# Own-segment blocks instead of full 128-key tiles in the token stage of a gated-attention backward kernel

## The chip, the cores and the metric

The kernel runs on one core of a Trainium2 chip. The metric is the device time of one execution in microseconds (us). A group of four heads of one 128-token tile, called a group below, is the unit of work in the stage that is changed.

## The reference, cut to what matters

The function returns the output of a gated sum of two attentions and the gradients of its inputs. Branch A is multi-query attention over 2048 tokens. Branch B is the one that the change touches: the 2048 tokens are cut into 64 segments of 32; each segment attends to itself (causally) and to 8 memory rows, and the attention's output at the memory rows becomes the memory of the next segment.

```python
M, seg = (8, 32)
for s in range(n_seg):
    h = jnp.concatenate([mem, xs], axis=1)
    q, k, v = (jnp.einsum('btd,dhe->bhte', h, W) for W in (Wq, Wk, Wv))
    scores = jnp.einsum('bhqe,bhke->bhqk', q, k) * scale
    p = _softmax(jnp.where(mask[None, None], scores, -1e9), axis=-1)
    o = jnp.einsum('bhte,hed->btd', jnp.einsum('bhqk,bhke->bhqe', p, v), Wo)
    mem = o[:, :M, :].copy()
```

There are 32 heads of 128 dimensions. Backward needs, for each head, P (the softmax), dP = dO V^T, dS = P (dP - delta) x scale with delta the row sum of P times dP, and then dQ = dS K, dK = dS^T Q, dV = P^T dO. The row sum of P times dP equals the row sum of dO times o.

## The kernel before, in words

The program goes through stages that follow one another on the core:

- preparation and projections, which write q, k, v and dO of all tokens to DRAM;
- the forward recurrence over 64 segments (memory rows only), woven with branch A's first pass;
- the token stage (`b_bulk`), which does the attention of the 2048 tokens, forward and backward up to dQ, now that all memories are known;
- the backward recurrence over 64 segments (`b_chain_bwd`), woven with branch A's second pass (`a_pass2`). Beside its own work it computes dK and dV of the last 11 token tiles (`kv_load`, `kv_mm`, `kv_out`, 176 products of four heads);
- the post stage (`b_post`): dK and dV of the other token tiles (`st_KV`), transposes (`st_T`) and the product with the transposed weights (`st_H`), 48 groups;
- the weight gradients (`b_dw`) and the rest of branch A.

Helpers record the instructions: `mm` (L82 of the profile) is every matmul and `tr` (L87) every transpose on TensorE, `evac` (L77 on VectorE, L79 on ScalarE) is a copy out of PSUM. `tp` is the position of a tile of the array: with weights of 128 rows by 32 columns, `tp=(0, 32c)` is one of four column tiles.

A 128-token tile holds four segments. In the token stage of before, a head's scores are a full matrix of 128 tokens by 128 keys, of which the four 32x32 blocks on the diagonal count, and beside it 128 tokens by 32 memory columns (four segments of 8), of which each token's own 8 count. After the exponential a mask of bits (`maskX`, 160 columns) sets everything else to zero. So `x_S` and `x_D` are 128x512 for four heads, `x_P` and `x_dS` 128x512, and `x_m`, `x_Pm`, `x_dSm` 128x128.

The stage runs 128 groups (16 tiles by 8) through a software pipeline that is written out by hand: the list `order` holds pairs of a lag and a step, and iteration t does each step for the group t minus its lag, in the list's order. The steps of before:

- `st_QT`, `st_KT`, `st_GT` (dO), `st_VT`: four transposes each on TensorE and one copy;
- `st_S` (L757 on): four matmuls of own keys, four of memory columns, two exponentials (L765, L766); `st_M`: the mask (L771); `st_R`: row sums (L778), reciprocal (L780), and P on GpSimd (L783, two operations);
- `st_T`: P transposed, 128x512 by 32x32 blocks on VectorE (L727) and the memory part by a transpose on TensorE;
- `st_O` with `attend`: the output of four heads: one matmul of 512 columns with a block-diagonal tile of memory rows (`x_vmB`), then four of 128, and a copy (L737);
- `st_OT`: o transposed, and `x_prod`, dO times o, on GpSimd (L806); `st_B`: the output projection, 8 matmuls of 288 columns, summed over a tile;
- `st_D`: dP, with delta subtracted inside PSUM by matmuls of `x_prod` with a tile of -1 (`negones`), then dS on VectorE (L842, two operations);
- `st_DT`, `st_Q`: as `st_T` and `st_O`, with dS and k; `st_K`: memory gradients, 16 matmuls every second group (L870 copies them).

`load` brings chunks of four groups from DRAM, `after` says behind which lag a chunk's next load is issued, `store` and `flush` put stores on SyncE's queue one iteration late. PSUM has eight banks: two buffers `x_tr`, one each of `x_S`, `x_po`, `x_D` and `x_m`, and two banks of `x_b`.

## Time and profile before

| what | value |
|---|---|
| median of three timed runs | 5509.4 us (5500.12 to 5520.96) |
| the profiled execution | 5481.23 us |
| its span, first to last instruction | 5479.5 us |
| mean granted TensorE clock | 0.982 |
| busy: TensorE (PE), VectorE (DVE), ScalarE (ACT), GpSimd (POOL) | 93%, 68%, 64%, 42% of the span |
| token stage, first transpose of q to the last copy of dQ | 2097 to 2778 us |
| the same, steady part, 2300 to 2500 us | 40 groups; PE busy 92%, DVE 83%, ACT 82%, POOL 53%, DMA engines 82% |

Times come from one profiled execution. The windows view gives each engine's busy time in a stretch of the span; the timeline gives starts and lengths of single instructions or runs of equal ones, with the shape of weights (rows times columns) and of the moving operand. A matmul's length is modelled and overlaps that of the next, so the distance between starts says what one costs.

### The profile page before, as it was taken

To read this page: it belongs to the slowest core of one execution; us is meant where nothing else is said; L and a number is where in the kernel's file an instruction comes from. 1 tells how busy PE (TensorE), PEld (TensorE's weight loads), DVE (VectorE), ACT (ScalarE), POOL (GpSimd) and SP (SyncE) were. 2 spreads that over 40 slices of the span, in tenths; PEclk is the share of its full clock that TensorE was granted. 3 is DMA by queue.
4 is the path that set the end of the run, shared out by engine and by line. 5 is a ranking of instruction groups with operands and counts; after the bars stand their busy time and mean duration, and the time that the engine had idled before them with its cause. 6 is when DMAs were issued, how large, how long until landed. Compare 5 with 4: busy or idle time off the path is not lost. (4 is left out here: it accounts for less than half of the span.)

```text
span 5479.5 us, 213173 instructions
## 1 busy us (share of the span) xinstructions
PE 5110.2 (93%) x90992; PEld 3046.4 (56%) x91173; DVE 3708.4 (68%) x6812; ACT 3496.5 (64%) x5264; POOL 2317.8 (42%) x4450
## 2 busy tenths in 40 slices
PE   8999999999999998999979999999998889999998
PEld 6435555555555556777735555555554457764444
DVE  5337888888888887888868888888888851111112
ACT  4327788888888886888857888788787742111001
POOL 4004555555555545555534454445444421122223
PEclk9999999999999998999989999999999999999999
DMA  6647667776675556888876899999986679976653
GB/s 216 230 175 139 139 133 138 144 136 137 140 140 123 119 105 189 258 254 255 250 242 168 202 210 207 204 211 211 204 193 137 147 165 281 265 225 219 199 174 108
DMA packets 1093581, 1013.05 MB, mean 185 GB/s; under 512 B 636979, under 2 KB 905788, under 8 KB 1083027
## 3 DMA queue, kind: packets, MB, share of 16 engines
q1 hardware_dynamic: 989010, 752.12, 57.2%
q0 software_dynamic: 100016, 242.38, 15.4%
q8 instruction: 713, 11.68, 0.9%
q10 hardware_dynamic: 3600, 4.90, 0.3%
q14 instruction: 242, 1.97, 0.1%
HBM read 547.90 MB, written 383.13 MB: 170 GB/s over the span
## 5 line engine op out<-in xcount | busy, mean ns | idle before, releaser
L1743 DVE TENSOR_TENSOR a_W<-a_dP,a_E 128x512 bf16<-128x512 f32 x2048 | 1315.0, 684 | 251.5 <-issue 118.6
L1889 DVE TENSOR_TENSOR b_dS<-b_dP,b_E 128x512 bf16<-128x512 f32 x2048 | 1311.6, 683 | 248.1 <-issue 115.0
L1866 ACT ACTIVATE b_E<-b_S 128x1024 bf16<-128x1024 f32 x1024 | 1049.1, 1024 | 299.8 <-PE b_dP L82 230.4
L1710 ACT ACTIVATE a_E<-a_S 128x1024 bf16<-128x1024 f32 x1024 | 1050.2, 1026 | 252.1 <-PE a_dP L82 166.7
L82 PEld LDWEIGHTS <-b_QS 32*128 32x128 bf16 (+1 forms) x8192 | 257.3, 92 | 553.2 <-issue 479.1
L82 PE MATMUL b_S<-b_KV,b_QS 32*128 32x512 bf16 x2048 | 406.3, 387 | 101.4 <-ACT b_E L1866 66.2
L82 PE MATMUL r_pj<-WT,r_dT 128*32 128x288 bf16 x12288 | 495.2, 288 | 5.1 <-issue 5.1
L82 PE MATMUL w_acc<-w_d,w_h 128*128 128x512 bf16 (+1 forms) x2352 | 471.0, 379 | 2.5
L82 PE MATMUL a_S<-a_QD,l_KV 32*128 32x512 bf16 x2048 | 401.6, 383 | 55.3 <-ACT a_E L1710 37.9
L82 PE MATMUL b_acc<-b_dS,b_QS 128*32 128x512 bf16 x2048 | 428.0, 396 | 0.9 <-issue 0.8
L82 PE MATMUL a_acc<-a_E,l_VK 128*32 128x256 bf16 x8192 | 403.8, 274 | 9.7 <-issue 5.5
L82 PE MATMUL b_acc<-b_E,b_QS 128*32 128x512 bf16 x2048 | 410.3, 396 | 0.1
L82 PE MATMUL b_dP<-b_KV,b_QS 32*128 32x512 bf16 x2048 | 405.2, 391 | 0.2 <-DVE b_dS L1889 0.2
L82 PE MATMUL a_dP<-a_QD,l_KV 32*128 32x512 bf16 x2048 | 400.6, 387 | 0.1
L82 PEld LDWEIGHTS <-r_dT 128*32 128x32 bf16 x12288 | 333.2, 97 | 101.2 <-issue 9.7
L82 PEld LDWEIGHTS <-w_h 128*128 128x128 bf16 (+1 forms) x2688 | 230.0, 100 | 258.2 <-issue 6.6
L82 PE MATMUL a_acc<-a_W,l_WK 128*32 128x256 bf16 x4096 | 305.6, 283 | 3.8 <-DVE a_W L1743 2.1
L82 PEld LDWEIGHTS <-l_KV 32*128 32x128 bf16 x4096 | 153.9, 91 | 261.6 <-issue 215.7
L79 ACT CAST w_o<-w_acc 128x512 bf16<-128x512 f32 x54 | 31.7, 586 | 384.2 <-PE w_acc L82 362.3
L783 POOL TENSOR_TENSOR x_P<-x_E,x_r 128x512 bf16<-128x512 bf16 x128 | 152.6, 1192 | 293.0 <-DVE x_r L780 290.5
L77 DVE CAST w_o<-w_acc 128x512 bf16<-128x512 f32 x54 | 37.3, 691 | 333.4 <-PE w_acc L82 306.8
L82 PEld LDWEIGHTS <-hm 128*32 128x32 bf16 x7680 | 201.7, 97 | 79.5 <-issue 11.7
(465 smaller groups left out, 10993.8 us busy)
## 6 DMA issues: line engine op xcount, KB each, us to landing
b_QS<-qs_dram SPq DMA_DIRECT2D x256, 256.0 KB
dOx_dram<-p_tok SPq DMA_DIRECT2D x16, 1024.0 KB
c_vx<-vx_dram SPq DMA_DIRECT2D x64, 256.0 KB
krow_dram<-c_k POOLq DMA_DIRECT2D x64, 256.0 KB
qrow_dram<-c_q POOLq DMA_DIRECT2D x64, 256.0 KB, 3.3
vrow_dram<-c_v POOLq DMA_DIRECT2D x64, 256.0 KB, 3.9
x_q<-qx_dram SPq DMA_DIRECT2D x32, 512.0 KB
x_k<-kx_dram SPq DMA_DIRECT2D x32, 512.0 KB
```

What stands on the lines that cost most here:

```text
L77: nc.vector.tensor_copy(out, in_)
L79: nc.scalar.copy(out, in_)
L82: return self.nc.tensor.matmul(out, lhsT, rhs, start=start, stop=stop, tile_position=tp, skip_group_check=True)
L783: nc.gpsimd.tensor_tensor(out=o[:, r, :], in0=Et[:, :, lo:lo + n], in1=rl[:].unsqueeze(2).to_broadcast([P, 4, n]), op=ALU.mult)
L1710: nc.scalar.activation(E_[n][:], S.pop(n)[:], ACT.Exp, scale=SCALEA)
L1743: nc.vector.tensor_tensor(out=W_[n][:, i, :], in0=dP[i][:], in1=E_[n][:, i, :], op=ALU.mult)
L1866: nc.scalar.activation(E_[n][:], S.pop(n)[:], ACT.Exp, scale=SCALEA)
L1889: nc.vector.tensor_tensor(out=D_[n][:, i, :], in0=dP[i][:], in1=E_[n][:, i, :], op=ALU.mult)
```

## The change

A head's scores, P and dS become 32 own keys and 32 memory columns, that is 2 x 32 columns a head in tiles `[P, 2, 4, 32]` (part, head, column). The own-key scores are computed as four 32-column tiles a head, each token segment against its own keys only. The mask has 2 x 32 columns. P^T and dS^T come from one transpose by blocks on VectorE, memory part included. The products P x V, dS x K and, in the later stages, dS^T Q and P^T dO are done by a new helper `diag_mm`: four matmuls on 32x32 tiles at the array's diagonal. Memory rows are loaded to partitions 40r to 40r+8 as whole rows. Delta is the row sum of P times dP times scale, taken on VectorE, and subtracted on GpSimd (`st_Y`); `x_prod` and the matmuls with -1 go from this stage. `st_B` is cut in two halves, the lags and the order of the steps are new, `x_po` has two buffers, `x_m` is gone (memory gradients share a bank with dP), and the loop has 7 extra iterations where it had 9. P and dS are kept in DRAM without their zero blocks.

```diff
-        self.px_dram = t("px_dram", [NTT, P, HB, P])
-        self.dsx_dram = t("dsx_dram", [NTT, P, HB, P])
+        self.px_dram = t("px_dram", [NTT, P, HB, SEG])
+        self.dsx_dram = t("dsx_dram", [NTT, P, HB, SEG])
...
+    def diag_mm(self, out, i, lhsT, rhs, start, stop):
+        for r in range(4):
+            b = slice(32 * r, 32 * r + 32)
+            self.mm(out[b, i, :], lhsT=lhsT[b], rhs=rhs[b], start=start, stop=stop, tp=(32 * r, 32 * r))
...
         def attend(o, PT, m, v):
-            po = psum.tile([P, 4, P], F32, name="x_po", bufs=1)
-            self.mm(po[:].rearrange("p i e -> p (i e)"), lhsT=PT[:, 512:640], rhs=m.rearrange("p i e -> p (i e)"),
-                    start=True, stop=False)
+            po = psum.tile([P, 4, P], F32, name="x_po", bufs=2)
             for i in range(4):
-                self.mm(po[:, i, :], lhsT=PT[:, 128 * i:128 * i + 128], rhs=v[:, i, :], start=False, stop=True)
+                self.diag_mm(po, i, PT[:, 0, i, :], v[:, i, :], True, False)
+                self.diag_mm(po, i, PT[:, 1, i, :], m[:, i, :], False, True)
             nc.scalar.copy(o, po[:])
...
+        def score(t, ps, l4, r4, w, part):
+            tt, g, r, d = view(t)
+            for i in range(4):
+                if part:
+                    self.mm(ps[:, 1, i, :], lhsT=l4[:, i, :], rhs=mT[tt][w][:, :, 4 * g + i, :])
+                    continue
+                for c in range(4):
+                    b = slice(32 * c, 32 * c + 32)
+                    self.mm(ps[b, 0, i, :], lhsT=l4[:, i, b], rhs=r4[:, i, b], tp=(0, 32 * c))
...
         def st_D(t):
...
+            ps = sc["D"][:, 0]
+            score(t, ps, sc.pop(("dOT", t)), sc.pop(("vT", t)), "v", 0)
+            X = sc["X", t] = sp.tile([P, 2, 4, 32], F32, name="x_X", bufs=2)
+            nc.vector.scalar_tensor_tensor(out=flat(X[:]), in0=flat(ps), scalar=SCALEB, in1=flat(d["P"][:, t % 4]),
+                                           op0=ALU.mult, op1=ALU.mult)
+            dl = sc["dl", t] = sp.tile([P, 4], F32, name="x_dl", bufs=2)
+            nc.vector.tensor_reduce(out=dl[:], in_=byh(X[:]), axis=AX.XY, op=ALU.add)
+
+        def st_Y(t):
+            tt, g, r, d = view(t)
+            Y = sp.tile([P, 2, 4, 32], F32, name="x_Y", bufs=1)
+            nc.gpsimd.tensor_tensor(out=Y[:], in0=d["P"][:, t % 4], in1=bc(sc.pop(("dl", t))[:]), op=ALU.mult)
+            o = chunk(t, "dS", [P, 4, 2, 4, 32], 3)
+            nc.gpsimd.tensor_tensor(out=o[:, t % 4], in0=sc.pop(("X", t))[:], in1=Y[:], op=ALU.subtract)
+            store(t, self.dsx_dram, o)
...
-        order = [(0, st_QT), (1, st_S), (3, st_T), (4, st_O), (0, st_KT), (2, st_R), (1, st_M), (5, st_OT), (5, st_VT),
-                 (6, st_D), (0, st_GT), (7, st_B), (8, st_DT), (9, st_Q), (7, st_K)]
+        order = [(0, st_QT), (2, st_GT), (3, st_T), (6, st_B0), (0, st_KT), (2, st_VT), (2, st_R), (6, st_B1), (5, st_OT),
+                 (4, st_Y), (5, st_DT), (1, st_Sm), (3, st_Dm), (1, st_S), (3, st_D), (6, st_K), (1, st_M), (4, st_O),
+                 (6, st_Q)]
...
-        for t in range(NG + 9):
+        for t in range(NG + 7):
```

In the backward recurrence `kv_mm`, and likewise `st_KV` in the post stage, does the token part first, by `diag_mm`, and the memory part after it:

```diff
             for i in range(4):
-                self.mm(pk[:, i, :], lhsT=kvS[rg, i, w, :], rhs=kvR[rg, w, i, :], start=True, stop=False, tp=(rg.start, 0))
+                self.diag_mm(pk, i, a[:, i, :], b[:, i, :], i == 0, False)
             for i in range(4):
-                self.mm(pk[:, i, :], lhsT=a[:, i, :], rhs=b[:, i, :], start=False, stop=True)
+                self.mm(pk[:, i, :], lhsT=kvS[rg, i, w, :], rhs=kvR[rg, w, i, :], start=False, stop=True, tp=(rg.start, 0))
```

In the forward recurrence two loops of eight matmuls, `c_v` by `PBm` and `c_vx` by `PBx`, become one loop that does both for each of the eight heads.

## The prediction

> **What bounds the kernel now.** I read the windows view first, to find the stages that the diff touches and what is busiest in each. Then the order of PE's instructions in them, since the change rewrites matmuls. The columns of the windows are: length, then busy time and count on PE, on the weight loader (PEld), DVE, ACT and POOL, then granted clock, DMA share, GB/s.

> ```profile
> 2300.00:2500.00 200.00, 183.90 (x2823) 152.17 (x2849) 166.33 (x362) 164.80 (x380) 105.75 (x120) 1.00 0.82 254
> 3000.00:4460.00 1460.00, 1375.19 (x29229) 739.14 (x29225) 1229.57 (x2136) 1154.85 (x1516) 675.74 (x1240) 0.99 0.87 190
> 4460.00:4690.00 230.00, 222.19 (x2319) 178.45 (x2320) 40.80 (x112) 54.84 (x101) 31.36 (x56) 0.96 0.94 249
> ```

> The first row is the token stage (2097 to 2778 us), the second the backward recurrence, the third the post stage. PE is the busiest engine in all three; DMA is high too. In the token stage the count of groups in the first window (40) gives 5.0 us a group; the first and the last transposes of q, 2097.0 and 2738.1, give 641.1 / 127 = 5.05 over the whole stage.

> The timeline of PE shows starts (first column) and modelled lengths. I go by starts: a length includes about 0.17 us of pipeline that the next matmul overlaps.

> ```profile
> 2500.72 0.38 PE L82 MATMUL x_po<-x_vmB,x_PT 128*128 128x512 bf16 x1
> 2500.94 0.39 PE L82 MATMUL x_po<-x_v,x_PT 128*128 128x128 bf16 x4
> 2501.16 0.39 PE L87 MATMUL x_tr<-identB,x_k 128*128 128x128 bf16 x4
> ...
> 2502.73 0.26 PE L82 MATMUL x_m<-x_vmT,x_dOT 128*128 128x32 bf16 x4
> 2502.83 0.25 PE L82 MATMUL x_m<-negones,x_prod 128*128 128x32 bf16 x4
> ...
> 2503.15 1.14 PE L82 MATMUL x_b<-WoN,x_oT 128*128 128x288 bf16 x8
> 2504.13 0.22 PE L87 MATMUL x_tr<-identB,x_dSm 128*128 128x128 bf16 x1
> 2504.41 0.39 PE L82 MATMUL x_po<-x_k,x_DT 128*128 128x128 bf16 x4
> 2504.72 0.25 PE L82 MATMUL x_m<-x_q,x_dSm 128*32 128x128 bf16 x4
> 2504.79 0.24 PE L82 MATMUL x_m<-x_dO,x_Pm 128*32 128x128 bf16 x4
> 2504.84 0.24 PE L82 MATMUL x_m<-x_q,x_dSm 128*32 128x128 bf16 x4
> 2504.90 0.24 PE L82 MATMUL x_m<-x_dO,x_Pm 128*32 128x128 bf16 x4
> 2505.07 0.40 PE L87 MATMUL x_tr<-identB,x_q 128*128 128x128 bf16 x4
> ```

> Prices from it: a full 128-column matmul 0.055 us (0.22 / 4), 512 columns 0.22, 288 columns 0.122 (0.98 / 8), full weights with 32 columns 0.027, a 128-column matmul on a 32-column tile 0.015 (0.18 for 12). A change of the tile shape costs 0.09 going in (2504.41 + 0.22 to 2504.72) and 0.11 going out.

> By these a group costs PE now: 20 transposes 1.10, S and D with `negones` 12 x 0.055 = 0.66, their memory columns 12 x 0.027 = 0.32, two memory transposes 0.11, P x V and dS x K 2 x (0.22 + 0.22) = 0.88, output projection 0.98, memory gradients and their switches every second group 0.22. Sum 4.27 us; the other 0.73 of the 5.0 is waiting (0.40 of it recorded as idle, PE busy 183.9 of 200; the rest behind modelled ends). So the stage is PE's work plus in-order waits, on evacuations for the most part.

> **The change, part by part, in the token stage** (128 groups).

> *Own-key scores.* S and D become 16 matmuls each, weights 128x32, 32 columns, on four column tiles. The nearest rows are in the backward chain:

> ```profile
> 3021.10 0.36 PE L82 MATMUL r_x<-r_dOT,r_vxT 128*32 128x8 bf16 x32
> 3021.31 0.42 PE L82 MATMUL r_x<-r_dOT,r_vmT 128*8 128x8 bf16 x32
> 3021.57 0.26 PE L82 MATMUL r_x<-r_prod,negones 128*32 128x64 bf16 x8
> ```

> 32 with 8 columns start within 0.21 us (0.007 each); 8 with 64 columns last 0.26, of which about 0.20 is one (0.009 each). With 128 columns it was 0.015. I take 0.009: 32 x 0.009 = 0.29 us, bounds 0.22 and 0.48.

> [...]

> *P x V and dS x K.* Each becomes 32 matmuls of 128 columns on 32x32 tiles at the diagonal (own keys, then memory), 64 a group. No 32x32 tile and no two row tiles writing one PSUM bank are in the trace of before, so this is the open price. Nearest from below: 128 columns on four column tiles, 0.015 (64 x 0.015 = 0.96 us, against 0.88 now). For row tiles side by side the chain has these:

> ```profile
> 3004.51 0.39 PE L82 MATMUL b_S<-b_KV,b_QS 32*128 32x512 bf16 x2
> 3004.52 0.39 PE L82 MATMUL b_dP<-b_KV,b_QS 32*128 32x512 bf16 x2
> 3004.84 0.39 PE L82 MATMUL b_acc<-b_dS,b_QS 128*32 128x512 bf16 x2
> ```

> Four row tiles start within about 0.01 us and the next work comes 0.33 later: they run together, though into different banks. From above: one after another, 0.055 (3.52 us). I take 0.015, since a diagonal tile shares neither rows nor output partitions with its three neighbours, and both kinds of neighbours are shown to overlap; the other end is a rival.

> *The rest on PE.* 20 transposes 1.10, projection 0.98 and memory columns 8 x 0.027 = 0.22 stay; memory gradients 8 x 0.015 = 0.12; `negones`, `prod` and the two memory transposes go. The new order puts all full-array work first, then column tiles, then diagonal tiles: three switches, 0.09 to 0.12 each, 0.32. Sum: 1.10 + 0.98 + 0.22 + 0.29 + 0.12 + 0.96 + 0.32 = **3.99 us** (bounds with the diagonal at 0.015: 3.92 and 4.18).

> *Other engines.* DVE per group now: transposes 0.70 and 0.70, reduction 0.81, mask 0.46, 0.68 + 0.28 for dS, two copies 0.42, reciprocal 0.18: 4.66. Halved lengths, by straight lines through the rows (0.28 at 128 and 0.68 at 512 elements give 0.41 at 256): 2 x 0.43 + 0.42 + 0.26 + 0.41 + 0.42 for the new delta sum + 0.85 + 0.18 = 3.4. ACT: five 512-element copies of 0.59 and two of 256 at about 0.38 = 3.7, from 4.7; the copies' starts can be 0.49 apart, so it holds a group in about 3.1. POOL: three operations at 0.66 (0.395 at 128, 1.196 at 512) = 2.0, from 2.7, of which two now stand between D and the store of dS, but with an iteration to spare. None of them passes PE.

> *DMA.* In the steady window the dynamic queue moved 34,483 packets and 50.36 MB at 81.7%, 76 ns a packet of 1,460 B; in 700 to 900 us it was 34.5 ns at 356 B. A line through both gives 21 ns + 0.037 ns a byte: 174 ns at 4,096 B, 31 ns at 256 B. Per four groups P and dS change 256 packets of 4,096 B for 1,024 of 256 B, and the memory rows 1,024 of 256 B for 64 of 4,096 B: 44.5 - 31.7 + 31.7 - 11.1 = 33 engine-us less, 0.5 us a group on 16 engines. DMA falls from 4.1 to 3.6 us a group: still under PE, but the next limit. SP issues as many transfers as before.

> *Waits.* Walking one iteration of the new order by these prices, the third transpose group has its buffer free (q copied out by 0.92 us, needed at 0.93), the fourth waits about 0.1 for ACT's copy of dO behind the copies of o and dq, the fifth none. The output buffer of the attention is doubled, which removes the wait between dS x K and P x V. I put waits at 0.25 in place of 0.73: **4.25 us a group**, bounds 4.0 and 4.7. Gain: (5.02 - 4.25) x 128 = 99 us, and two iterations fewer in the tail, at some 4 us, 8 us.

> **Other stages.** Post stage (48 groups, 4.48 us from start to start, all PE): 8 full matmuls (0.44) become 32 diagonal ones (0.48) and one more switch (0.1): 0.14 x 48 = +7 us; its smaller loads of p and dS free DMA, which only two short waits ask for. Backward chain: 176 products, 4 full matmuls (0.22) become 16 (0.24), but the products now end in the shape of the next matmul, b_S, so a switch goes: -0.08 x 176 = -14 at most. Its steps come every 1.555 us, set by b_S, the exponential (1.03 us) and b_S's single buffer, so I count 0, bounds -14 and +10. In the forward chain the pairs are only interleaved: eight matmuls of 0.027 now stand behind one POOL result, whose waits now add up to 1.7 us in 64 steps; I count 0, bounds 0 and +12. Masks and constants at the start: three short POOL operations, under 2 us.

> **Sum.** -99 - 8 + 7 = -100 us. The profiled execution took 5481.2 us (span 5479.5), the median of the three timed runs is 5509.4, 28 above; the sum goes to 5381 for a profiled run, and 5409 against the median.

> **Rivals.**
> 1. *Diagonal tiles run one after another.* Then 0.055 for each: token stage 64 x 0.040 = +2.56, so 6.8 us a group, +228 us against now; chain 16 x 0.040 x 176 = +113, since those steps are already full; post stage 32 x 0.040 x 48 + 7 = +68. About 5509 + 228 + 113 + 68 - 8 = 5910. It decides from 0.027 a matmul on (64 x 0.012 = 0.77 eats the gain): at 0.0275, two at a time, the time is about 5509 + 4 + 35 + 26 - 8 = 5566. For: no row shows row tiles in one bank. Against: the overlap rows above. Chance 0.14.
> [...]
> 2. *The waits stay.* PE gets lighter, yet two transpose buffers and ACT's order keep 0.7 us: 4.7 us a group, -41 - 8 + 7 = -42, 5467. For: five evacuations still share two buffers. Against: the walk above. Chance 0.12.
> 3. *DMA takes over.* Stage at 4.9 to 5.0 us a group because small packets cost twice my line: 5490 to 5510. Against: under 0.5 us of 200 went to DMA waits. Chance 0.08.
> Forecast: 0.66.

> Faster by over 0.5% (27 us; about what a measurement can tell): forecast and rival 2, 0.78. Within: rival 3, 0.08. Slower: rival 1, 0.14. The range runs from period 4.0 without loss elsewhere (-130 - 8 - 14 = -152, near 5355) to rival 3 (5500).

> **What would show it.** Steps: 16 diagonal matmuls of one tile within about 0.24 us; S and D starts 0.007 to 0.015 apart; period 4.25; PE idle under 0.3 us a group; DMA share near 0.85. Wrong if the x_po groups last 1.8 us each, or if a group of transposes is regularly preceded by a wait over 0.3 us.

## The result, and the profile after

The changed kernel is slower: 5591.7 us, the median of four timed runs (5581.83 to 5613.6), against 5515.2 for the kernel before timed beside it (5500.12 to 5524.32). The ratio is 1.0147, with a 95% interval of 1.0105 to 1.0189. The forecast was 5409 us.

The windows view of the profiled execution (span 5580.1 us, clock 0.975), in the columns used before. The first window is the same steady part of the token stage; the other two are shifted by 80 and 100 us, since the later stages now begin about 100 us later:

```profile
2300.00:2500.00 200.00, 158.28 (x5033) 131.60 (x5033) 120.15 (x327) 124.97 (x255) 68.95 (x108) 0.95 0.64 191
3080.00:4540.00 1460.00, 1376.51 (x31144) 735.70 (x31132) 1231.55 (x2136) 1156.76 (x1518) 675.72 (x1235) 0.99 0.84 180
4560.00:4790.00 230.00, 226.94 (x3528) 178.42 (x3517) 41.62 (x115) 55.32 (x103) 32.26 (x58) 0.98 0.84 209
```

In the token stage every engine is busy for less of the time than before, and so is DMA. The stage lost its bound and became slower: something waits. The counts of PE and PEld rose from some 2,830 to 5,033 each. From the first transposes of q to the last, the stage takes 711.4 us where it took 641.1: 5.60 us a group instead of 5.05.

The other stages moved little. Between the spans lie 100.6 us, for the most part:

- +70 in the token stage;
- +28 ahead of it, 27 of them in the forward recurrence (1674.5 us against 1647.7);
- +4 in the backward recurrence (1641.2 against 1637.1);
- nothing in the post stage (218.4 against 218.9).

The timeline of PE in the steady part (start, length, operation, shape of weights, shape of the moving operand, count; in brackets the idle time ahead and what ended it):

```profile
2399.89 0.24 PE L82 MATMUL x_S<-x_kT,x_qT 128*32 128x32 bf16 x10
2401.63 0.22 PE L82 MATMUL x_S<-x_kT,x_qT 128*32 128x32 bf16 x6 [1.49 <-issue]
2401.68 0.27 PE L82 MATMUL x_D<-x_vT,x_dOT 128*32 128x32 bf16 x16
2402.53 0.24 PE L82 MATMUL x_D<-x_q,x_dS 128*32 128x128 bf16 x4 [0.58 <-DVE x_X L846]
2402.59 0.24 PE L82 MATMUL x_D<-x_dO,x_P 128*32 128x128 bf16 x4
2402.76 0.23 PE L82 MATMUL x_po<-x_v,x_PT 32*32 32x128 bf16 x4
2402.82 0.23 PE L82 MATMUL x_po<-x_vmB,x_PT 32*32 32x128 bf16 x4
2402.88 0.23 PE L82 MATMUL x_po<-x_v,x_PT 32*32 32x128 bf16 x4
...
2403.61 0.23 PE L82 MATMUL x_po<-x_kmB,x_DT 32*32 32x128 bf16 x4
2403.76 0.40 PE L87 MATMUL x_tr<-identB,x_q 128*128 128x128 bf16 x4
...
2406.33 0.27 PE L82 MATMUL x_S<-x_kT,x_qT 128*32 128x32 bf16 x16
2406.45 0.26 PE L82 MATMUL x_D<-x_vT,x_dOT 128*32 128x32 bf16 x16
2407.32 0.24 PE L82 MATMUL x_D<-x_q,x_dS 128*32 128x128 bf16 x4 [0.62 <-DVE x_X L846]
```

Three things are to be read here. The diagonal tiles are cheap: groups of four start 0.055 us apart, 0.014 a matmul. There is a wait in nearly every iteration (114 times in 2100 to 2800 us): the memory gradients of `st_K` write the tile `x_D` while VectorE (`x_X`, L846) still reads dP in the other half of it. And there is a hole of 1.49 us in the middle of 16 equal matmuls, which waits for nothing that the profile knows. The largest waits of PE, 2300 to 2500 us (total us, times, longest us):

```profile
PE x_D L82 <- DVE x_X L846: 23.2, 36, 1.0
PE x_tr L87 <- issue: 5.1, 2, 3.1
PE x_tr L87 <- DVE x_kT L77: 4.6, 9, 0.5
PE x_po L82 <- issue: 3.8, 4, 1.6
PE x_S L82 <- issue: 2.2, 2, 1.5
```

In the kernel before the token stage has no wait of the "issue" kind on PE. After has 35 of them with 52.9 us in 2100 to 2800 us. (For every kernel below, such holes are counted in this window for the token stage's tiles.)

**Where the holes lie.** They are at one place of the instruction stream, not of the program. Number PE's instructions in the order of the trace (two for each weight load with its matmul, one for each semaphore instruction). All 35 holes of after then stand at an index that leaves 194 on division by 256, and so do all of k_last (64), k_tr (68), split (32), nomem (19) and light (48), the kernels of the next section; in hyb 32 of 36 stand at 194 or 195. So PE stops where one block of 256 instructions ends and the next begins. The DMA queues of before and of after in 2300 to 2500 us (packets, MB, share of the 16 engines):

```profile
q1 hardware_dynamic: 34483, 50.36, 81.7%
q8 instruction: 22, 0.36, 0.7%
```

```profile
q1 hardware_dynamic: 27106, 37.60, 62.8%
q8 instruction: 38, 0.62, 1.3%
```

A packet of the instruction queue is 16.4 KB, which for 256 instructions is 64 bytes each. Over the whole execution after moves 806 such packets; PE's 103,056 matmuls and 103,141 weight loads make 805.5 blocks of 256. Before it was 713 for 711.6. So this queue carries PE's instructions, and the change nearly doubled what it has to bring in the token stage.

The trace also shows when a block comes. There is one packet a block, in order, and it starts about when PE enters the block ahead of it or later. In after (2150 to 2650 us) the start comes 2.0 us behind that entry at the median, and over 3.8 us behind it in one case of ten; the packet then takes 1.0 us, and PE begins no block sooner than 1.2 us after its packet has landed. That makes 4.2 us at the median and 6 in the late cases, where 256 instructions last 4.4 us at the pace of an undisturbed iteration. In before the delays are much the same (1.9 and 4.3 us), but a block lasts 8.9 us, so none is late.

**What a hole leaves behind.** A hole costs more than its own length, because TensorE's granted clock drops behind many of the long ones. Three windows of after, around the longest hole (columns as above; the clock is the third number from the end):

```profile
2293.60:2298.30 4.70, 0.30 (x5) 0.21 (x3) 0.77 (x2) 0.31 (x1) 0.00 (x0) 1.00 0.67 201
2298.30:2301.70 3.40, 2.89 (x19) 2.04 (x17) 1.26 (x4) 1.17 (x2) 0.88 (x2) 0.50 0.50 180
2301.70:2306.00 4.30, 3.65 (x138) 3.10 (x136) 2.10 (x6) 2.81 (x6) 1.04 (x2) 1.00 0.12 32
```

In the second window four projection matmuls take 0.87 us (2298.18 to 2299.05) that take 0.49 elsewhere. Behind its first 45 us, the token stage of after has 15 such drops, 72 us in all at a granted clock of 0.5; each began with PE idle for 1.7 us or more of the 3.4 us ahead. The same part of before has none.

### The profile page after: what moved, and what is told of

Same layout as the page of the kernel before. It is cut to its first block, busy times and chain, and to the rows that moved or that the text cites. A ratio compares the mean times of both kernels' runs of the same rounds, so it can differ in the third digit from the quotient of the medians.

```text
span 5580.1 us, 237075 instructions
## 1 busy us (share of the span) xinstructions
PE 5102.7 (91%) x103056; PEld 3020.0 (54%) x103141; DVE 3599.7 (65%) x6813; ACT 3407.3 (61%) x4944; POOL 2228.4 (40%) x4453
## 5 line engine op out<-in xcount | busy, mean ns | idle before, releaser
L1878 ACT ACTIVATE b_E<-b_S 128x1024 bf16<-128x1024 f32 x1024 | 1048.2, 1024 | 302.2 <-PE b_dP L82 216.9
L82 PEld LDWEIGHTS <-b_QS 32*128 32x128 bf16 (+1 forms) x8192 | 267.4, 92 | 541.9 <-issue 495.1
L82 PE MATMUL r_pj<-WT,r_dT 128*32 128x288 bf16 x12288 | 492.3, 286 | 11.3 <-issue 11.2
L82 PE MATMUL b_S<-b_KV,b_QS 32*128 32x512 bf16 x2048 | 406.1, 385 | 89.1 <-ACT b_E L1878 65.0
L82 PE MATMUL w_acc<-w_d,w_h 128*128 128x512 bf16 (+1 forms) x2352 | 470.9, 379 | 2.5
L82 PE MATMUL a_S<-a_QD,l_KV 32*128 32x512 bf16 x2048 | 404.1, 385 | 49.3 <-ACT a_E L1722 35.5
L82 PE MATMUL b_acc<-b_dS,b_QS 128*32 128x512 bf16 x2048 | 426.5, 395 | 2.9 <-issue 1.5
L82 PE MATMUL a_acc<-a_E,l_VK 128*32 128x256 bf16 x8192 | 407.0, 276 | 9.3 <-issue 5.1
L82 PE MATMUL b_acc<-b_E,b_QS 128*32 128x512 bf16 x2048 | 408.9, 395 | 0.4 <-issue 0.4
L82 PE MATMUL b_dP<-b_KV,b_QS 32*128 32x512 bf16 x2048 | 406.5, 390 | 2.8 <-issue 2.6
L82 PE MATMUL a_dP<-a_QD,l_KV 32*128 32x512 bf16 x2048 | 402.6, 389 | 0.1
L82 PEld LDWEIGHTS <-r_dT 128*32 128x32 bf16 x12288 | 330.5, 97 | 107.7 <-issue 16.1
L82 PEld LDWEIGHTS <-w_h 128*128 128x128 bf16 (+1 forms) x2688 | 229.8, 100 | 258.4 <-issue 6.6
L82 PE MATMUL a_acc<-a_W,l_WK 128*32 128x256 bf16 x4096 | 306.4, 284 | 6.0 <-issue 5.4
L82 PEld LDWEIGHTS <-l_KV 32*128 32x128 bf16 x4096 | 149.8, 91 | 263.5 <-issue 222.3
L794 POOL TENSOR_TENSOR x_P<-x_E,x_r 128x256 bf16<-128x256 bf16 x128 | 78.5, 614 | 442.8 <-ACT x_vT L79 295.2
L82 PEld LDWEIGHTS <-hm 128*32 128x32 bf16 x7680 | 202.7, 97 | 79.6 <-issue 11.2
```

Of the source, the lines that this page charges most:

```text
L82: return self.nc.tensor.matmul(out, lhsT, rhs, start=start, stop=stop, tile_position=tp, skip_group_check=True)
L794: nc.gpsimd.tensor_tensor(out=o[:, t % 4], in0=Et[:], in1=bc(rl[:]), op=ALU.mult)
L1878: nc.scalar.activation(E_[n][:], S.pop(n)[:], ACT.Exp, scale=SCALEA)
```

## The experiments

Two theories are tested, and they need not exclude each other. **Tile**: the wait of `st_K` for VectorE, 0.61 us in every iteration, is the loss. **Supply**: 280 PE instructions a group, where there were 145, are more than is brought in time beside the stage's transfers; the time at half clock is counted to it where it follows a hole. A third, **forward recurrence**: the interleaved loop costs the 28 us ahead of the stage.

The table gathers the runs. "Instructions" are PE's in a group, as built. "Undisturbed" is the lower quartile of the distance between iterations. "Wanted" is instructions by that distance, the rate that the iteration asks for while nothing is late. "Half clock" is the time at a granted clock of 0.5 in the stage behind its first 45 us.

| kernel | ratio to before | token stage, us | instructions | undisturbed, us | wanted, per us | DMA share | holes, us (count) | half clock, us |
|---|---|---|---|---|---|---|---|---|
| before | 1 | 641 | 145 | 4.94 | 29 | 0.82 | 0 | 0 |
| hyb3 | 0.9983 [0.9967, 1.0000] | 636 | 200 | 4.79 | 42 | 0.72 | 4 (9) | 7 |
| nomem | 0.9978 [0.9962, 0.9993] | 615 | 216 | 4.50 | 48 | 0.76 | 16 (19) | 20 |
| hyb | 0.9917 [0.9888, 0.9946] | 627 | 224 | 4.46 | 50 | 0.75 | 34 (36) | 20 |
| split | 1.0149 [1.0121, 1.0177] | 701 | 260 | 5.02 | 52 | 0.76 | 31 (32) | 14 |
| after | 1.0147 [1.0105, 1.0189] | 711 | 280 | 4.80 | 58 | 0.64 | 53 (35) | 72 |
| k_tr | 1.0182 [1.0150, 1.0214] | 728 | 280 | 4.42 | 63 | 0.62 | 112 (68) | 140 |
| k_last | 1.0140 [1.0108, 1.0173] | 694 | 280 | 4.15 | 67 | 0.66 | 107 (64) | 92 |
| light | 0.9840 [0.9809, 0.9871] | 562 | 280 | 4.03 | 69 | 0.41 | 37 (48) | 0 |

In k_tr even the lower quartile is disturbed: its 33 iterations with neither a hole nor half clock take 4.04 us at the median, as long as light's, and ask for 69 instructions per us.

### k_last and k_tr: take the wait on the tile away

k_last does the memory gradients behind `st_Q`, when VectorE has long read dP:

```diff
-                 (4, st_Y), (5, st_DT), (1, st_Sm), (3, st_Dm), (1, st_S), (3, st_D), (6, st_K), (1, st_M), (4, st_O),
-                 (6, st_Q)]
+                 (4, st_Y), (5, st_DT), (1, st_Sm), (3, st_Dm), (1, st_S), (3, st_D), (1, st_M), (4, st_O),
+                 (6, st_Q), (6, st_K)]
```

> The changed kernel with the memory-gradient step moved from between dP and P x V to the end of an iteration, behind dS x K; nothing else moves. In the changed kernel its first matmul stands 0.61 us idle behind VectorE's reading of dP, which lies in the same PSUM tile, and it does so in each of the 128 groups. Theory A (that wait is a large part of the loss): the idle goes, one more change of tile shape costs about 0.11, the undisturbed iteration falls from 4.79 to about 4.3 us, and with stalls as they are the time falls by 0.5 x 128 = 64 us against the changed kernel, to about 5530. Theory B (TensorE now lacks instructions: all gaps put down to issue fall on a boundary of 256 instructions): the undisturbed iteration falls all the same, but 256 instructions then last 3.9 us in place of 4.4, the gaps grow, and less than half of the 64 us arrives. Rival (the wait only covers the copies that follow): the iteration stays at 4.7 to 4.8 with the idle time before another step.

k_tr keeps the order and gives the gradients one of the transposes' buffers:

```diff
-            pk = sc["D"][:, 1].rearrange("p w i k -> p (w i k)").rearrange("p (x e) -> p x e", e=P)
+            pk = psum.tile([P, 2, P], F32, name="x_K", tag="x_tr", bufs=2)
...
-            sc["D"] = psum.tile([P, 2, 2, 4, 32], F32, name="x_D", bufs=1)
+            sc["D"] = psum.tile([P, 1, 2, 4, 32], F32, name="x_D", bufs=1)
```

> The changed kernel with the memory gradients in a buffer of the transposes' PSUM rotation in place of the other half of the bank of dP; the order of the steps is unchanged. If it is the shared tile that makes the step wait, the 0.61 us before it go without a further change of shape: undisturbed iteration 4.2 us, against 4.3 with the step moved. If the step waits for its own operands, the 0.61 stay. The theory of missing instructions expects the same limited gain in time as with the step moved, or less, since the instructions come faster still.

k_last took 5562.2 us (1.014), k_tr 5588.4 (1.018). In both the wait on `x_X` is gone, and an undisturbed iteration falls from 4.80 to 4.15 and 4.42 us. The stage hardly follows: 694 and 728 us. The holes and the half clock took the freed time. The largest waits of PE in k_last, 2300 to 2500 us:

```profile
PE x_po L82 <- issue: 12.7, 6, 3.5
PE x_D L82 <- issue: 8.7, 6, 3.0
PE x_tr L87 <- DVE x_kT L77: 4.6, 9, 0.5
PE x_tr L87 <- issue: 2.7, 4, 0.9
PE x_S L82 <- issue: 2.3, 1, 2.3
```

Its instruction queue brought 40 packets in these 200 us against 38, hardly faster for an iteration that could run 0.65 us shorter. So the tile theory names a real wait of 0.61 us a group, 73 us in all, but taking it away is worth at most 17 us of the stage, and nothing that the whole time shows (1.0140 and 1.0147 can't be told apart); behind it stood the next limit. In k_tr PE's granted clock in the window is 0.87 (0.95 in after), which adds to its time.

### split: only more instructions

This is the kernel before, with the same arithmetic cut into more matmuls: the projection in pieces of 72 columns instead of 288, the own-key scores, dP, delta and P x V, dS x K and the memory gradients in 64 instead of 128, the memory product in four. No tile shape, wait or transfer of the change is in it. One of the cuts:

```diff
-                self.mm(Sp[:, i, :], lhsT=qT4[:, i, :], rhs=kT4[:, i, :], start=(i == 0), stop=True)
+                for z in (0, 64):
+                    self.mm(Sp[:, i, z:z + 64], lhsT=qT4[:, i, :], rhs=kT4[:, i, z:z + 64], start=(i == 0 and z == 0), stop=True)
```

> The kernel before with 58 more matmuls a group in the token stage and the same arithmetic: the output projection in pieces of 72 columns, S, dP, its delta part and the products of own keys in pieces of 64, the memory product in four pieces, the memory gradients in pieces of 64. By the rows of before the pieces cost TensorE the same as the whole (0.027 each for 0.055 or 0.122 in four), so the undisturbed iteration stays near 5.0 to 5.1 us, but a group has 260 instructions and weight loads in place of 145, near the 280 of the changed kernel. Theory of missing instructions: gaps put down to issue appear in this stage, where before had none, each at a multiple of 256 instructions, and the stage grows by 25 to 80 us. Rival (the gaps of the changed kernel come from its waits, its data transfers or its small tiles): no such gaps, time within 15 us of before.

It took 5567.6 us, 1.015 times before: the stage grew by 60 us, with 31 us in 32 holes where before had none, at the same place of the block. More instructions alone make the holes. Of the other 29 us, 10 are the undisturbed iteration (0.08 longer) and at most 7 the 14 us at half clock; the rest is not itemised.

### pairs: the forward recurrence

Before, with only the interleaved loop:

```diff
-            for u in range(8):
```

> The kernel before with only the edit of the forward chain: the two loops of eight matmuls become one. In the profile of the changed kernel this stage is 27 us longer than before, though the commonest step is 25.24 us in both. If the edit is the cause: +20 to +30 us against before. If the 27 us are the scatter of the stage's sporadic gaps from one execution to another: within 8 us of before, steps still 25.24 us at their commonest.

5496.3 us against 5494.0 by the medians; the ratio is 1.0020 (1.0002 to 1.0037), which is 11 us, with 1 to 20 possible. So the edit may cost something, but little. In the profiled executions the forward recurrence took 1661.8 us here, 1648 to 1675 in the kernels that have the edit, and 1647.7 and 1656.9 in before and split, which don't. Its commonest step is 25.25 to 25.26 us in before, after and pairs. The 28 us ahead of the token stage therefore lie within the scatter between executions; how many of them are the edit's is not shown.

### nomem and light: fewer instructions, and fewer transfers

nomem is after without the 32 matmuls of the memory part in P x V and dS x K, so o and dQ lack the memory's part:

```diff
-                self.diag_mm(po, i, PT[:, 0, i, :], v[:, i, :], True, False)
-                self.diag_mm(po, i, PT[:, 1, i, :], m[:, i, :], False, True)
+                self.diag_mm(po, i, PT[:, 0, i, :], v[:, i, :], True, True)
```

> The changed kernel without the 32 diagonal matmuls a group that add the memory rows in P x V and dS x K (so o and dQ lack the memory's part). TensorE's sum falls by 32 x 0.014 = 0.45 us a group, the undisturbed iteration from 4.79 to about 4.34, and the instructions from 280 to 216 a group, so 256 of them last 5.1 us in place of 4.4. Theory of missing instructions: the gaps put down to issue shrink from 57 us in the stage to under 25, and the mean iteration falls by more than the work, from 5.6 to about 4.6: 120 us less than the changed kernel. Rival (gaps come with the small tiles or with transfers): gaps as before, mean iteration 5.6 - 0.45 = 5.15, 58 us less.

The stage took 615 us, 96 less than after, between the 120 of the supply theory and the 58 of its rival. The holes shrank by 36.5 us, and the time at half clock by 51, which is at most 26 us of PE's work. The matmuls left out are worth 32 x 0.014 x 128 = 57 us, but the undisturbed iteration fell by only 0.30 us, 38 in all, because other waits grew (that on the copy of dO by 14 us, that on the copy of k by 8). The wait on `x_X` stayed, 81.7 us in 125 times.

light is k_tr without the loads of q, k, v and dO after the first chunks; later chunks compute on what lies there:

```diff
+                    z = c % 4 if w in deep else c % 3
+                    if c != z:
+                        d[w] = kept[w, z]
+                        continue
...
+                    kept[w, z] = d[w]
```

> The kernel with the memory gradients in the transposes' PSUM rotation (no 0.61 us wait, 71 gaps and 118 us put down to issue in the stage), with the loads of q, k, dO and v left out after the first four (v: three) chunks, so that later chunks compute on old data; half of the stage's DMA bytes go. Instructions and order stay. If instruction blocks arrive late because they share the 16 DMA engines with the data: gaps shrink to less than half, the mean iteration falls from 5.7 to under 5.0. If a block of 256 instructions takes its 5 us whatever the load: gaps stay near 110 us and the iteration at 5.5 to 5.7. If the loads themselves held TensorE up: the named DMA waits go, which are 2.4 us in 200.

It has k_tr's instructions, 280 a group, and only the transfers are fewer (k_tr first, then light):

```profile
2300.00:2500.00 200.00, 163.30 (x4855) 135.87 (x4857) 115.81 (x317) 118.96 (x248) 66.96 (x105) 0.87 0.62 188
2300.00:2500.00 200.00, 187.54 (x6392) 159.38 (x6394) 155.44 (x418) 154.64 (x326) 87.04 (x137) 1.00 0.41 132
```

The DMA share is down from 0.62 to 0.41, PE's busy time up from 163 to 188, its matmuls from 4,855 to 6,392. The stage takes 562 us, 166 less than k_tr. The holes fall from 112 to 37 us, and the half clock from 140 us, at most 70 us of work, to none. A typical iteration (the median) is 4.14 us. So the work of the changed stage is what was forecast (3.99 us of PE work); what fails is bringing its instructions beside the data. Holes and clock explain up to 145 of the 166 us. Of the rest, 26 us are shorter waits on the copies of q and k; waits on data are no large part, since PE's waits on DMA in k_tr's stage add up to 2.4 us.

The packets tell how the transfers act. An instruction packet takes 1.0 us in light as in k_tr, but it starts 1.2 us behind PE's entry into the block ahead at the median, against 2.2 in k_tr; one in ten starts later than 1.9 us in light and later than 4.4 us in k_tr. So a block comes late because its packet starts late, and fewer data transfers make it start sooner.

### hyb, hyb2, hyb3: keep the cheap parts, spend fewer instructions

hyb is k_tr with the memory part of P x V and dS x K done as before, one matmul of 512 columns with the block-diagonal tile, and its two transposes on TensorE with one copy; the own part stays in diagonal tiles. The memory rows are loaded in small pieces again, as before. 224 instructions a group.

```diff
+        def st_Om(t, z="P", m="v"):
+            po = sc[z + "po", t] = psum.tile([P, 4, P], F32, name="x_po", bufs=2)
+            self.mm(po[:].rearrange("p i e -> p (i e)"), lhsT=sc.pop((z + "M", t)),
+                    rhs=mB[m][t // 4 % 2][:, t % 4].rearrange("p i e -> p (i e)"), start=True, stop=False)
...
-                self.diag_mm(po, i, PT[:, 0, i, :], v[:, i, :], True, False)
-                self.diag_mm(po, i, PT[:, 1, i, :], m[:, i, :], False, True)
+                self.diag_mm(po, i, PT[:, i, :], v[:, i, :], False, True)
```

> A candidate for a better kernel: the memory part of P x V and dS x K as in the kernel before (two transposes on TensorE in one PSUM buffer, one copy, one matmul of 512 columns with the block-diagonal memory rows each), the own part as four diagonal tiles a head, memory gradients in the transposes' rotation. 224 instructions a group in place of 280; TensorE's sum is 3.99 - 0.48 + 0.44 + 0.11 = 4.06, so the undisturbed iteration should be 4.2 to 4.4, and 256 instructions last 4.8 to 5.0 us. Theory of missing instructions: gaps between those of the kernel with nothing but the wait removed (118 us) and none, mean iteration 4.7 to 5.1, time from 40 us under before to 10 over. Rival (instructions are not the limit): mean iteration 4.3 to 4.5, 70 to 95 us under before.

5450.2 us against 5488.1 for before on the same chip: 0.9917 (0.9888 to 0.9946), faster than both kernels. An undisturbed iteration is 4.46 us, and the stage 627 us with 34 us of holes.

hyb2 stores P and dS in rows of 1,024 bytes instead of 256, so that there are fewer packets:

```diff
-            o = chunk(t, "P", [P, 4, 2, 4, 32], 3)
-            nc.gpsimd.tensor_tensor(out=o[:, t % 4], in0=Et[:], in1=bc(rl[:]), op=ALU.mult)
+            o = chunk(t, "P", [P, 2, 4, 4, 32], 3)
+            nc.gpsimd.tensor_tensor(out=o[:, :, t % 4], in0=Et[:], in1=bc(rl[:]), op=ALU.mult)
```

> The candidate with the memory part as before (224 instructions a group, 36 gaps and 34 us put down to issue, mean iteration 4.92), with the chunks of P and dS laid out so that a store is 128 pieces of 1,024 B in place of 512 of 256 B. Instructions unchanged. Theory of instruction blocks delayed by data on the same DMA engines: some 16 engine-us less in each chunk of about 330, so a little shorter gaps, 0 to 15 us under that candidate. Rival (transfers do not matter in this way): equal within 5 us.

0.9955 (0.9937 to 0.9974): packets fell from 43,269 to 34,842 in 200 us, the stage from 627 to 620, the holes not at all (34.3 us in both). The intervals of hyb and hyb2 overlap and hyb2's ratio is the higher one, so no gain is shown. A fifth fewer packets did nothing for the holes.

hyb3 takes 24 more instructions out of hyb2: dP's own part as four full matmuls a group, of which VectorE then picks the blocks in four pieces:

```diff
+            for i in range(4):
+                self.mm(ps[:, i, :], lhsT=l4[:, i, :], rhs=r4[:, i, :], start=(i == 0), stop=True)
...
+            for c in range(4):
+                b = slice(32 * c, 32 * c + 32)
+                nc.vector.scalar_tensor_tensor(out=X[b, 0], in0=ps[b, :, b], scalar=SCALEB, in1=d["P"][b, 0, t % 4],
+                                               op0=ALU.mult, op1=ALU.mult)
```

> The same, with dP's own part as four full matmuls a group in place of 16 on column tiles (the scaling on VectorE then in four pieces of 32 partitions and one for memory): 200 instructions a group, 256 of them last 5.6 us at 4.4 us a group. TensorE's work changes by under 0.1 us, VectorE's rises from 2.8 to about 3.8 us a group, still under 4.4. Theory of missing instructions: gaps fall from 34 us to 10 to 20, mean iteration 4.6 to 4.7, time 20 to 35 us under the kernel with the 1,024 B pieces, some 60 to 75 under before. Rival (what is left are waits on VectorE and ScalarE): mean iteration stays at 4.8 to 4.9.

0.9983 (0.9967 to 1.0000): the holes are almost gone, 4 us, as the supply theory wants. But the time missed its forecast of 60 to 75 us under before: the four pieces cost VectorE 1.19 us, and a new wait took the holes' place; of hyb3's PE waits, 2100 to 2800 us:

```profile
PE x_tr L87 <- DVE x_qT L77: 60.9, 113, 3.7
PE x_tr L87 <- DVE x_kT L77: 15.2, 19, 6.0
```

PE now waits for the copy of q in nearly every iteration, 0.54 us each, and an undisturbed iteration is 4.79 instead of 4.46.

## Why the prediction was wrong, point by point

**What failed: the step "waits at 0.25 in place of 0.73".** Two terms are missing in it, and the second brought a third with it.

1. *The wait of `st_K` on dP's tile.* The walk through the iteration went by the transposes' buffers and left out that the memory gradients share a tile with dP, though the text of the change says so. It costs 0.61 us a group. The undisturbed iteration of after is 4.80; without that wait it would be 4.19, against the forecast 4.25, and light, which has no such wait, has 4.03 to 4.14. So the walk's other numbers hold. No run tried the step without the wait in the same tile; k_last moved it behind `st_Q` and k_tr took another buffer, and in both the wait on `x_X` is gone.
2. *The supply of instructions* was in no term of the sum and in none of the rivals. From 4.80 undisturbed the mean went to 5.60 us a group. Of the 0.80, 0.42 are holes recorded as such (52.9 us over 127 groups) and 0.1 a wait for `x_kT` in 24 of the groups. That the supply is the cause and not a companion: split makes the holes with nothing but more instructions; nomem loses 36.5 us of them with 64 instructions fewer; light loses 75 us of them with the same instructions and fewer transfers; all of them in after stand at one place of a block of 256; and at the median they end 1.4 us after an instruction packet has landed.
3. *The clock.* The sum took every price at full clock. 72 us of the stage ran at a granted clock of 0.5, behind holes for the most part: up to 36 us lost, 0.28 a group, about what the 0.80 still lacked. Before has no such time in the steady stage, and light none.

The missing terms are not additive. Each alone looks like 50 to 80 us, but with the wait gone the iteration asks for 67 instructions per us instead of 58, the holes doubled from 53 to 107 us, and the half clock grew from 72 to 92. That is why k_last gives so little.

**The step on diagonal tiles** was right: 0.014 measured for 0.015, and 16 within 0.22 us for "within about 0.24". Rival 1 is out: four row tiles wrote disjoint partitions of one tile, `x_po`, side by side, at 0.014 us each and not at its 0.055.

**Own-key scores**: 16 within 0.12 us, 0.0075 each for 0.009. **Switches**: 0.08 to 0.11 us each (2399 to 2409 us in after) for 0.09 to 0.12. **PE's work**: light's 4.03 is 0.04 above 3.99.

**Other engines**: right. VectorE's transposes by blocks last 0.42 to 0.435 us (0.43 forecast), dP times P 0.42 (0.41), delta's sum 0.42, GpSimd's operations 0.61 to 0.73 (0.66). None of them is busy enough to limit: VectorE 60%, ScalarE 62% and GpSimd 34% of the steady window.

**DMA**: 62.8% of 5.60 us is 3.5 us a group, for 3.6; 74 ns a packet of 1,387 bytes, for 72 by the line. Rival 3 was wrong as put: of PE's waits in 2100 to 2800 us one, of 4.8 us, is on DMA, at a DMA share of 0.64 in the steady window. What hurts is that instruction packets start late beside the data (2.2 us behind PE's entry into the block ahead in k_tr, 1.2 in light). The expected share of 0.85 failed with the period it was divided by.

**Rival 2** (waits stay, 4.7 us a group, 5467) came nearest to the undisturbed iteration of 4.80, though by another wait than the one it named.

**Post stage**: +7 forecast, -0.5 measured; no run shows which of its prices was off. **Backward recurrence**: 0 forecast, +4 measured, within its bounds. **Forward recurrence**: 0 forecast; the profile showed +27, of which pairs leaves 1 to 20 to the edit. **Tail**: -8 forecast; from the last transposes of q to the last copy of dQ it took 33.6 us for 40.8, so -7.

**The rival on the slow side** was one mechanism, the diagonal tiles, with a chance of 0.14. The real one could have been seen coming in the trace of before, though not priced: the instruction queue's line stood in its profile with 22 packets in the window, the doubling of PE's count per group was known, and its packets already started up to 5 us behind PE's entry into the block ahead. At 8.9 us a block that was harmless (no hole); at 4.4 it was not (35 holes in after).

**What stays open**: why a block's packet starts late. The delay depends on the transfers (2.2 us in k_tr, 1.2 in light), but whether the packet waits behind data in the engines' queues, or is asked for late, the trace does not tell; hyb2 speaks against the plain number of packets (34.3 us of holes with a fifth fewer). The recurrence's window in after asks for 62,276 instructions in 1460 us, 43 per us at a DMA share of 0.84, and costs only 4 us more than before, which fits hyb3's 42 with hardly a hole.

## What to carry to other kernels

When a change cuts matmuls into smaller tiles, count PE's instructions per us, weight loads too, and compare with what the profile shows to run without "issue" holes; here 42 per us ran nearly clean (4 us of holes) beside a DMA share of 0.72, 48 to 52 began to fail (16 to 34 us), and 67 lost 107 us of a stage of 694. Count the granted clock to the price of an idle stretch: here a hole of 2 us often cost 3.4 us or more at half clock behind it (after: 15 drops, 72 us). A new step that wrote into a PSUM tile waited here for the reader of the tile's other half, 0.61 us a group in after: walk the order by tiles, not only by the buffers that rotate. Small tiles cost TensorE less here where they save columns: 16 tiles of own-key scores start within 0.12 us in after, where four full matmuls took 0.22 in before. The memory part, one matmul of 512 columns in 0.22 us, took 0.22 in 16 diagonal tiles too, and was better left whole: that mix, hyb, is the version that is faster than both, by 0.8% against before.
